# One recurrent-attention and feed-forward kernel, its written order, load queues, engines and PSUM banks changed

## The chip, the core and the metric

The kernel runs on one core of one Trainium2 chip. The metric is device time in microseconds (us), the median of several executions. One more execution was taken by the hardware profiler; its span runs from the first to the last instruction. The engines are called as in the profile: PE (matmul; PEld is its weight load), DVE, ACT, POOL and SP. SP computes nothing and only issues transfers; "ACTq", "SPq" and "POOLq" are the issuing of transfers by ACT, SP and POOL.

## The reference

Two parts follow each other. With batch 4, 8 heads, 768 steps and head size 48:

```python
for t in range(S):
    cur = einsum(u * k[t], v[t])                     # per batch and head, 48 x 48
    y[t] = einsum(r[t], state + cur)
    state = w[t][..., None] * state + einsum(k[t], v[t])
...
h = x @ w_in                                         # x is y: 3072 tokens x 384; w_in 384 x 1024
sm = softmax(h); solu = h * sm
ln = (solu - mean(solu)) / sqrt(var(solu) + 1e-6) * g_ln
out = ln @ w_out                                     # 1024 x 384
```

All inputs and the output are float32.

## The kernel before

The steps are cut into 6 chunks of 128; a chunk of one batch is a *unit*. There are 24 units, number 4c + b for chunk c and batch b. Each unit passes the same stages, each a short word in a text that is called ORDER: the word's letters name the stage, its digits the unit, and what follows the dot names an engine, a queue or a PSUM bank.

- Loads: `LW`, `LK`, `LR`, `LV` bring w, k, r and v of one unit, 192 KB each, as 1024 runs of 192 bytes. `LI0` to `LI2` bring the thirds of w_in (512 KB each), `LO0` and `LO1` the halves of w_out (768 KB each). With no letter SP issues the transfer, with `.a` ACT, with `.g` POOL (line 120). Each of w, k and r, v has a ring of 7 buffers, so a load of unit i waits until unit i - 7 has been used.
- Attention: `lw` (ACT, logarithm of w), `cum` (PE, running sums), `ex` (ACT, exponentials in PSUM), `kp` (DVE, k and r scaled by them), `krk` and `krr` (PE, transposes), `kr` (their copy, on ACT or DVE), `M` (PE, scores) and `m` (masked copy), `S`, `et`, `st` (state), `p`, `q`, `dg`, `dv` (the term with u; POOL and DVE), `vb` (v in bfloat16), `Y` and `y` (attention output), `X` and `xT` (its transpose).
- Feed-forward: `H` (PE, 24 matmuls with w_in), `e` (ACT, exponential), `he` (DVE, h * e), `hq` (its square), `Oa` and `Ob` (PE, the product with w_out in two halves, and column sums), then small steps and `o`, `out` (the store). The weights are prepared once: `wi` casts w_in, `gw` scales w_out by the gain in 8 parts (0 to 3 are the half of `LO0`), `mn` and `mc` make the column mean, `ce` subtracts it, part by part. `Oa0` needs `ce` of parts 0 to 3. `hot` is a run of matmuls without use for the result.
- Late units (16 to 23) take some transposes by transfer (`kt`, `xt`, `ht`, all from SP).

No loop sets the order. Lines 593 to 596 walk through ORDER and issue each word as it stands there; line 84, which the profile names for nearly all instructions, is the helper that records each engine's instructions in just that order:

```python
for word in ORDER.split():
    word, _, how = word.partition(".")
    name = word.rstrip("0123456789")
    stages[name](int(word[len(name):]), how)
```

So an engine never passes over an instruction that waits. That holds for issuing too: a load with `.a` stands in ACT's stream between ACT's computations (line 270 is `load_w_out`, line 501 `hidden_exp`, the stage `e`).

One more order is made by the build and is not written in ORDER. A transfer that SP or ACT issues counts its landing on one of eight semaphores, DMAHW0 to DMAHW7. Before the next transfer on the same semaphore is issued, its engine waits until the earlier one on it has landed. POOL's transfers have semaphores of their own. Which transfer stands on which semaphore is seen in the built program; the parts that the steps below touch are, for this kernel:

```
DMAHW3: LR0 LK2.a LK4.a LR7.a LV7 LR10.a LW15 ...
DMAHW4: LW2.a LW3 LK5 LR6 LI1.a LW13 LR12 ...
DMAHW0: LW0 LR2 LK1 LW7 LR9 LK10 LR14.a ...
DMAHW2: LW1.a LV1 LR5 LW8 LK9 LW14 LK14 LW11.a ...
DMAHW7: LK0.a LR3 LW9.a LR8.a LI0.a LR11 ...
```

PSUM has 8 banks; the digit after the dot of a PE word is its first bank. `cum`, `M` and `H` take two banks. A PE word waits until the earlier contents of its banks have been read.

Of the kernel before, what the change touches and what calls it, by code (L numbers as in the profile page):

```python
# [36 lines left out]
ex11 dv8 q10 kp11 lw13 sq1 Y8.n6 krr14 qm1 qm0 ex12 H4.3 lv0 y8.d kp12 vb11.p lv1 ea3.p rs1 rs0 vb10.p ea2.p LR17
p12 o0.d sel10 krk11.6 o1.a cum13.0 kr14.d out1 dg9 hq2.a ex13 krr11 Oa3.2 kr11.d e4 out0 vb12.p q12 krk12.7 kp13
Ob3 lw15 sq3 lw17 LR16.a Oa2.5 cum15.0 krr12 qm3 he4 LK17.a p11 LK15 dv9 q11 krk13.6 Ob2 ex15 S10.3 S11.4 p14 lv3
LW21 kr12.d LV16.a rs3 kp15 LK16 LK19 sq2 et10 o3.a qm2 et11 Y9.i7 krr13 lv2 cum17.0 st10 lw16 y9.a rs2 st11 ex17  # L40
o2.a out3 ea4.p S12.2 kr13.d cum16.3 dg11 et12 H5.6 kp17 p15 ex16 st12 kp16 e5 hq4.a p13 dg10 X8.5 LW19 H7.0 vb13.p
e7 he5 H6.2 out2 e6 LV18.g dg12 he7 dv10 S13.4 LK18 Oa4.7 he6 et13 krk15.6 LR20 lw19 hq5.a Ob4 q13 M12.0 xT8.a sq4
krr15 LV15.g st13 dv12 m12.a qm4 qh13 Y10.n3 Oa5.2 M11.0 M13.4 Ob5 lv4 rs4 sel12 kr15.d LV17 o4.a q14 LV14 vb14.p
X9.7 m11.a hq6.d y10.d q15 X10.3 LW18 LR19 sq5 M14.0 m13.d ea6.p lw18 LK20 dv11 xT9.d qm5 LR22.a cum19.4 lv5 xT10.d
hq7.d rs5 H8.6 m14.d sel11 dg13 dv13 o5.a ex19 e8 LK22.a kp19 H9.2 out4 ea7.p Oa6.0 cum18.4 LW20 he8 e9 Ob6 LR18
S14.6 Y11.n7 lw20 ea9.p ex18 he9 sq6 p16 qm6 kp18 out5 lv6 H10.1 rs6 o6.d hq9.a et14 dg14 st14 e10 dv14 Y12.n4
Oa7.0 y11.d LW22 y12.d vb16.a cum20.5 hq8.a ex20 q16 Ob7 ea8.p LK21 sq7 kt16 vb15.a dg15 he10 kt17 lw22 kp20 qm7
p17 Y14.n3 Oa9.7 X11.4 xT11.a lv7 q17 out6 y14.d rs7 S16.2 Y13.n1 ea10.p y13.d et16 Ob9 o7.a M15.3 sq9 kt18 st16
qm9 m15.a M17.0 LW23 M18.5 Oa8.2 m17.d M16.3 lv9 cum22.0 rs9 o9.a vb17.a LK23 out7 p19 LV21 hq10.a ex22 out9 m18.d
Ob8 m16.d qh16 dg16 LV19 dg17 kt19 H11.5 sq8 lw21 Oa10.3 X12.4 p20 e11 qm8 kp22 xT12.a lv8 X13.7 xT13.d dv15 he11  # L50
dv17 sel15 q20 Ob10 rs8 sq10 q19 o8.a qm10 lv10 rs10 out8 X14.4 H12.0 Y17.n7 Y15.n2 xT14.d e12 dv16 hq11.a H13.5
e13 o10.d ea11.p y15.d he12 y17.d LR23 p18 out10 LV22 he13 vb18.p ea12.p hq12.a H14.3 Y16.n7 LR21 Oa11.0 q18
cum21.1 Ob11 e14 qh19 y16.d ex21 vb19.d he14 sq11 p22 hq13.a S15.6 qm11 kt22 lv11 rs11 dg18 dv18 o11.a Oa12.7 et15
X15.5 Ob12 ea13.p kt20 sq12 kp21 M19.3 xT15.d p23 qm12 xt16 lv12 st15 Y18.n2 H15.0 rs12 out11 ea14.p LV23 o12.a
dg20 m19.d lw23 e15 y18.d ea15.p dg19 he15 H16.6 dv19 out12 Y19.n5 cum23.2 Oa13.4 vb23.p hq14.a xt17 kt21 S17.0
ex23 kp23 q23 Ob13 p21 q22 LV20 xt18 vb21.a e16 sq13 Oa14.1 qm13 H17.2 kt23 lv13 y19.d et17 rs13 o13.a he16 sv16
vb20.p M21.4 hq15.a e17 M20.6 st17 out13 Ob14 sq14 dg23 m20.d Oa15.0 dv23 qm14 vb22.p m21.a S19.7 Ob15 xt19 he17
ht16 q21 lv14 rs14 o14.a sel21 sq15 qm15 lv15 et19 M23.3 m23.d out14 dv20 M22.1 ht17 rs15 H18.5 qh21 m22.a dg21
o15.a out15 e18 dv21 Y20.n4 y20.d dg22 xt20 hq16.a Y21.n2 S18.1 et18 y21.d dv22 hq17.a sel22 he18 H19.3 xt21 st18
Oa16.0 Oa17.2 e19 st19 ht18 hq18.a Y22.n1 Ob16 sq16 y22.d Ob17 he19 qm16 lv16 xt22 sq17 H21.5 sv18 Y23.n7 qm17  # L60
Oa18.4 sv17 rs16 lv17 rs17 e21 o16.d ht19 hq19.a o17.d H20.0 y23.d out16 e20 Ob18 sq18 out17 he21 xt23 H22.5 qm18
# [565 lines left out]
```

## Time and profile before

| what | value |
|---|---|
| median of 3 executions | 156.16 us (154.19 to 156.34) |
| profiled execution's own time | 151.6 us |
| its span | 149.7 us |
| mean granted PE clock | 0.966 |
| busy: PE, DVE, ACT, POOL | 130.6, 122.3, 122.1, 116.0 us |
| moved by transfers | 31.50 MB, mean 210 GB/s |

The page gives, in tenths, how busy each engine was in 40 equal slices of the span, the clock granted to PE, and the mean busy share of the 16 DMA engines. The view of windows gives busy time by engine in stretches that one names. The timeline lists instructions with start and duration; a bracket at a line's end gives the idle time before it and what ended it.

### The profile page before, as it was taken

Reading aid. Unit: us, or ns where it says so; the run is one execution under the profiler, and the core shown is the slowest. Engines: PE = TensorE matmul, PEld = TensorE weight load, DVE = VectorE, ACT = ScalarE, POOL = GpSimd, SP = SyncE. Lnnn points to the kernel's source line nnn. Section 1 sums busy time; section 2 is a strip of 40 time slices with the busy share of each in tenths; the row PEclk is TensorE's granted clock in tenths of the full one; section 3 lists DMA queues with packets and bytes.
Section 4 is the critical chain, followed back from the end, with each engine's and each line's share of the span. In section 5 each row is a group of like instructions: output and inputs, shape, how many; then the busy total and the mean of one; then the engine's idle time right before and its main releaser. Section 6 shows DMA issues by size and latency. Waiting matters only on the chain. (4 is left out here: it accounts for less than half of the span.)

```text
span 149.7 us, 4668 instructions
## 1 busy us (share of the span) xinstructions
PE 130.6 (87%) x1804; PEld 95.3 (64%) x1809; DVE 122.3 (82%) x211; ACT 122.1 (82%) x266; POOL 116.0 (77%) x147
## 2 busy tenths in 40 slices
PE   6957439787599989999999999999999999899970
...
PEclk9999975899959999999999999999999999999999
DMA  5999999999999899989998999895978687479342
GB/s 104 255 287 262 278 239 210 246 286 316 362 322 254 174 204 226 204 215 246 244 239 180 224 220 217 174 203 146 198 184 185 119 194 210 100 173 166 88 158 105
DMA packets 112199, 31.50 MB, mean 210 GB/s; under 512 B 107161, under 2 KB 111266, under 8 KB 112178
## 3 DMA queue, kind: packets, MB, share of 16 engines
q1 hardware_dynamic: 91426, 24.26, 74.1%
q10 hardware_dynamic: 20048, 4.79, 14.3%
q0 software_dynamic: 704, 2.16, 4.4%
...
## 5 line engine op out<-in xcount | busy, mean ns | idle before, releaser
L84 PE MATMUL ps<-w,he 128*128 128x385 bf16 x192 | 42.4, 325 | 0.7 <-DVE st L84 0.4
L84 DVE TENSOR_TENSOR kp<-ps,kr_in 128x768 bf16<-128x768 f32 x24 | 22.9, 952 | 11.0 <-ACT ps L84 6.9
L84 POOL TENSOR_TENSOR p<-kr_in 128x384 bf16<-128x384 f32 x24 | 23.9, 1003 | 4.6 <-DMA kr_in<-in_k_dram 3.6
L84 PE MATMUL ps<-xT,win_sb 128*128 128x128 bf16 x432 | 27.0, 220 | 0.0
L84 POOL TENSOR_TENSOR ea<-e 128x512 bf16<-128x512 bf16 x15 | 17.7, 1184 | 11.0 <-ACT e L84 11.0
L84 PEld LDWEIGHTS <-win_sb 128*128 128x128 bf16 x432 | 25.2, 99 | 0.7
L84 ACT ACTIVATE e<-ps 128x1024 bf16<-128x1024 f32 x24 | 24.4, 1020 | 0.9 <-PE ps L84 0.8
L84 ACT ACTIVATE ps<-ps 128x768 f32<-128x768 f32 x24 | 19.1, 802 | 6.1 <-PE ps L84 6.0
L84 PE MATMUL ps<-one_col,hq 128*128 128x1 bf16 x144 | 23.6, 164 | 0.0
L84 DVE TENSOR_TENSOR he<-ps,e 128x1024 bf16<-128x1024 f32 x18 | 21.7, 1216 | 1.5 <-ACT e L84 1.4
L84 POOL TENSOR_TENSOR q<-p,u_bc 128x384 bf16<-128x384 bf16 x24 | 22.5, 939 | 0.2
L84 PEld LDWEIGHTS <-he 128*128 128x128 bf16 x192 | 18.0, 96 | 7.1 <-DMA he<-win_f 1.3
L84 DVE TENSOR_TENSOR m<-ps,keep 128x1024 bf16<-128x1024 f32 x18 | 21.7, 1216 | 0.4 <-PE ps L84 0.4
L84 POOL TENSOR_TENSOR dv<-vb,dg 128x384 bf16<-128x384 bf16 x24 | 19.9, 832 | 1.9 <-DVE dg L84 1.2
L84 PEld LDWEIGHTS <-kp 128*128 128x128 bf16 x208 | 13.9, 101 | 6.2 <-DVE kp L84 2.2
L84 ACT ACTIVATE lw<-w_in 128x384 bf16<-128x384 f32 x24 | 12.4, 525 | 4.2 <-DMA w_in<-in_w_dram 4.2
L84 PEld LDWEIGHTS <-kr 64*128 64x128 bf16 (+1 forms) x272 | 11.0, 97 | 6.2 <-issue 2.7
L84 PEld LDWEIGHTS <-hq 128*128 128x128 bf16 x144 | 11.2, 96 | 5.6
L84 ACT ACTIVATE hq<-he 128x1024 bf16<-128x1024 bf16 x13 | 13.7, 1053 | 0.0
L84 PE MATMUL ps<-ident,kp 128*128 128x128 bf16 x128 | 11.6, 231 | 1.6 <-DVE kp L84 1.6
L84 DVE TENSOR_REDUCE dg<-q 128x8 f32<-128x384 bf16 (+1 forms) x24 | 11.9, 500 | 0.4 <-POOL q L84 0.4
L84 PE MATMUL ps<-lw,uti_neg 128*128 128x384 bf16 x24 | 8.2, 344 | 3.2 <-DVE m L84 1.2
...
## 6 DMA issues: line engine op xcount, KB each, us to landing
...
```

The costliest lines, as they stand in the source:

```text
L84: made = make(*args, **kwargs)
```

## The change

Only ORDER is written anew. All stages are the same, and the sizes of the rings too. What differs:

- Loads by queue: of the 96 loads of w, k, r, v, SP issues 71 (66 before), ACT 19 (as before, but other ones, 16 of them ahead of `e0` where it was 12) and POOL 6 (11 before). All five transfers of w_in and w_out (`LI`, `LO`) come from ACT; before, ACT issued `LI0` and `LI1` and SP the rest.
- The order of the loads and of the units (`kp` runs 0 1 2 3 6 4 5 7 8 9 10 13 11 12 ... instead of 0 1 2 3 5 4 7 6 8 9 10 14 11 12 ...).
- Engines: `kr` 13 on DVE and 3 on ACT (10 and 6), `m` 16 and 8 (18 and 6), `xT` 6 and 10 (10 and 6), `o` 11 and 13 (8 and 16), `vb` 14 on POOL and 10 on ACT (11 and 12, one on DVE), `gw` 3 on POOL and 5 on ACT (1 and 6, one on DVE), all three `wi` on POOL (2, one on ACT), small shifts of `ce`, `y`, `sel` and `qh`.
- `hot`: 20 matmuls in six words instead of 18 in four. PSUM banks are given anew.

The start of ORDER, up to the first words of the feed-forward part:

```diff
-LW0 ih0 LW1.a LW2.a LU0 LR0 LG0 LK0.a lw0 hot13.0 cum0.0 LR1 LK1.a LR2 LK2.a ex0 LV1 LW3 LV2.g LW4 LW5 ik0 lw2 kp0
-us0.4 lw1 p0 cum1.5 LR3 LK3 uc0 ex1 cum2.0 kp1 ex2 LV3.g krk0.2 p1 kp2 q0 hot3.3 krk1.6 vb1.a LV0.a krr0 lw3 LR5
...
-xT1.a vb6.a st1 S3.1 M4.2 LI1.a X0.0 q5 kp7 et3 p6 cum6.4 xT0.d gs0.7 p7 ex6 Y2.i6 dg4 m4.d S4.0 gc0 vb8.a M5.2 LV7
-lw8 kp6 Y3.i7 y2.a q6 LI2 krk7.4 st3 y3.a dv4 krk6.5 vb5.a cum8.6 et4 m5.d LI0.a S5.1 st4 ex8 dg5 cum9.2 LO1 ex9
-krr6 krr7 LK10 kp8 q7 kp9 kr6.a krk8.0 et5 p8 krr8 wi1.p dg6 lw10 kr7.d X2.5 vb7.p LR10.a xT2.a kr8.a S6.6 Y4.i3
-dg7 X3.5 xT3.d S8.7 et6 st5 y4.a dv5 LO0 S7.5 et8 et7 wi2.a LW14 st6 M6.3 Y5.i2 st8 M7.6 cum10.0 LW13 dv7 m6.d
-wi0.p y5.a m7.d LR14.a ex10 X4.2 LV9.g st7 H0.3 xT4.d krk9.5 LV10 q8 LW12 qh8 LR11 gw7.a gw5.a dv6 LV13.g H1.6 LK12
-LK14 kp10 e0 gw6.a Y6.n0 he0 krk10.1 krr9 X5.2 gw4.a gw2.d e1 gw0.a krr10 gw1.a gw3.p p10 y6.d xT5.d he1 kr9.d p9
...
+LR0.a LK0.a LW0 LR1.a LW1 lw0 hot10.0 cum0.0 lw1 cum1.2 LV0.a ex0 ex1 LR3.a LV3.g ik0 kp0 LV5.g LV4.g LU0 LR2.a LK1
+vb3.a us0.4 LW2 LV2.g LW3 uc0 lw2 lw3 LK3.a LV6.g ih0 LV1 kp1 p0 krk0.7 krr0 kr0.d krk1.0 vb0.a LW6 krr1 vb1.a
+kr1.d M0.3 cum2.6 m0.d M1.0 ex2 LW4.a hot2.2 cum3.2 S0.4 m1.d lw6 LW5.a LK2 LV7.g LK6 q0 cum6.0 ex3 kp2 ex6 p1 p2
+dg0 kp3 S1.5 hot5.6 krk3.2 krk2.3 et0 krr3 krr2 LR6 st0 LW7 vb2.p vb5.a kp6 LR4.a vb4.a et1 dv0 q2 p3 LR5 st1
+krk6.4 lw4 krr6 Y0.i5 LK5.a LK7.a cum4.6 lw7 lw5 ex4 LK4 LW8 kr3.d kr2.d y0.a LR7 kr6.d dg2 S2.0 et2 q1 q3 cum7.3
+cum5.1 LK8.a dg1 dv1 p5 ex5 S3.5 kp4 krk4.7 LW13 LI2.a krr4 st2 vb6.a X0.6 kp5 p6 ex7 hot1.0 M3.0 vb7.p p4 xT0.a
+et3 dg3 kr4.d q5 q4 LW9 dv2 m3.a sel3 dv3 qh5 S5.2 LK10 kp7 M4.6 m4.d lw13 LK9.a S4.3 LG0 krk5.4 lw9 LR8 et5 Y1.i1
+krr5 lw8 et4 st3 st5 gs0.7 kr5.d LW14.a M2.5 st4 m2.d LW10 p7 dg4 dv4 y1.a hot1.0 X1.4 lw10 LI1.a xT1.a gc0 cum8.0
+cum9.2 ex8 ex9 hot1.4 krk7.5 krr7 LR10 LR9 q7 wi2.p LW11 lw11 cum10.6 S7.4 ex10 LI0.a kp8 Y3.i0 Y2.i1 y2.a kr7.d
+kp9 kp10 et7 st7 LW12 dg5 krk8.5 cum13.2 krr8 y3.a lw12 LR13 X3.1 lw14 X2.0 LK13 M5.6 xT3.a xT2.a M6.0 ex13 LK12.a
+LV9 LK11 kr8.d p10 dv5 p8 m5.d wi1.p Y4.i4 M8.5 krk9.7 kp13 m6.a LV10 krr9 LO1.a M7.0 S6.2 wi0.p y4.a m8.d m7.d
+kr9.a et6 cum11.3 LR11 cum12.5 Y5.i7 ex11 LR12 ex12 st6 y5.a H0.0 X4.7 kp11 LV8 vb10.a sel6 q8 q6 krk10.4 LO0.a e0
+M9.2 vb8.p vb9.p kp12 xT4.a dg7 LK14 m9.d krr10 H2.5 LW15 kr10.a p11 qh8 LR14 LV11 X5.7 he0 dv7 H1.2 krk11.0 LV13
+dg6 q10 dv6 gw7.p krk13.4 e2 LW16 he2 gw4.a gw0.p e1 krr11 Y7.i1 cum14.5 LW20 kr11.d krr13 xT5.a krk12.7 S9.0 y7.a
+he1 kr13.d gw6.a gw1.p S8.1 ex14 gw5.a dg8 krr12 kp14 et8 Y6.n2 et9 LK17 LR15 H3.3 kr12.a gw2.a LV14 gw3.a X7.7
+LW17 e3 st9 dv8 st8 vb11.p M11.5 Y8.n0 xT7.d mn0.1 p9 m11.a y6.d mc0 S11.2 lw15 ce6.d he3 ce1.p ce0.p ce4.d ce2.d
+ce5.d LK15 et11 LK16 M12.5 H4.3 ce3.p st11 m12.a ce7.d M10.5 krk14.7 hq0.a q9 hq1.a S10.2 Oa0.1 hq3.a LV12 lw16
...
```

The semaphores of the changed program are given out anew by the build. Those on which ACT's loads stand:

```
DMAHW1: LW1 LV0.a LW7 LW13 LK7.a LK13 LI1.a LW16 ...
DMAHW2: LR0.a LV1 LK3.a LW9 LR10 LV9 LV8 LW20 LO0.a LK18 ...
DMAHW3: LU0 LW6 LR5 LR4.a LR9 LK11 LK14 LK12.a ...
DMAHW4: LK0.a LK2 LK4 LK10 LK8.a LK9.a LW15 ...
DMAHW6: LR1.a LK6 LW8 LR8 LW12 LW14.a LI0.a LO1.a LW18 ...
DMAHW7: LW2 LR2.a LR7 LK5.a LI2.a LR11 ...
```

The built program has, in ACT's stream, `LO0.a` directly ahead of `e0`, and `LO0.a` waits on DMAHW2 until eight transfers on it have landed, the eighth of which is `LW20`.

More of the change, by code (lines that the diff above doesn't have):

```diff
@@ L27 @@
-dg3 krk4.3 Y1.i6 LR8.a p5 krk5.7 lw9 krr4 krr5 cum7.4 dv3 m3.d y1.a X1.6 ex7 q4 LV5.g kr5.a kr4.d dv2 LR9 LK8 LK9
-xT1.a vb6.a st1 S3.1 M4.2 LI1.a X0.0 q5 kp7 et3 p6 cum6.4 xT0.d gs0.7 p7 ex6 Y2.i6 dg4 m4.d S4.0 gc0 vb8.a M5.2 LV7
-lw8 kp6 Y3.i7 y2.a q6 LI2 krk7.4 st3 y3.a dv4 krk6.5 vb5.a cum8.6 et4 m5.d LI0.a S5.1 st4 ex8 dg5 cum9.2 LO1 ex9
-krr6 krr7 LK10 kp8 q7 kp9 kr6.a krk8.0 et5 p8 krr8 wi1.p dg6 lw10 kr7.d X2.5 vb7.p LR10.a xT2.a kr8.a S6.6 Y4.i3
-dg7 X3.5 xT3.d S8.7 et6 st5 y4.a dv5 LO0 S7.5 et8 et7 wi2.a LW14 st6 M6.3 Y5.i2 st8 M7.6 cum10.0 LW13 dv7 m6.d
@@ L32 @@
-wi0.p y5.a m7.d LR14.a ex10 X4.2 LV9.g st7 H0.3 xT4.d krk9.5 LV10 q8 LW12 qh8 LR11 gw7.a gw5.a dv6 LV13.g H1.6 LK12
-LK14 kp10 e0 gw6.a Y6.n0 he0 krk10.1 krr9 X5.2 gw4.a gw2.d e1 gw0.a krr10 gw1.a gw3.p p10 y6.d xT5.d he1 kr9.d p9
-dg8 kr10.a LW15 H3.3 e3 mn0.0 mc0 LR12 ce6.d Y7.i2 hq0.a H2.5 vb9.p y7.a lw14 ce4.d he3 ce0.p ce3.d ce2.d M10.1
-LW11.a ce7.p ce5.p M9.3 S9.7 m10.a et9 m9.d ce1.p LK11 st9 LR15 cum14.0 e2 lw12 hq1.a he2 LV11.g Oa0.2 M8.3 Ob0
-X7.7 ex14 m8.d LV12 kp14 q9 hq3.d lw11 xT7.a Oa1.5 LW16 LR13.a cum11.3 X6.7 Ob1 xT6.d LK13 sq0 LW17 cum12.0 krk14.7
@@ L37 @@
[L37 to L61, printed above, removed]
@@ new lines @@
+krr14 LW21 Ob0 LW18 sel11 p12 m10.d sel12 et10 sq0 q11 y8.d dg9 LR16 Oa1.0 e4 LW19 ea2.p dg10 qm0 cum16.5 LR17 lv0
+kr14.d lw17 p13 st10 Ob1 rs0 ex16 sq1 Oa3.7 hq2.a he4 o0.d cum15.3 LK18 q12 qm1 dv10 Ob3 kp16 ex15 cum17.1 out0 sq3
+lv1 ex17 qm3 lv3 p15 ea4.p H5.5 LV16 kp15 kp17 rs1 dv9 rs3 o1.a q13 o3.d Oa2.3 X6.4 krk15.0 Ob2 e5 p16 xT6.d hq4.a
+Y10.n2 sq2 vb12.a X8.1 he5 qm2 lv2 dg11 rs2 o2.a krr15 Y9.n7 LV15 dg12 H6.4 dv11 Y11.n3 out1 lw21 y9.d vb14.p dv12
+kr15.d xT8.a p14 q15 out3 M14.0 vb13.p lw19 e6 ea6.p LK20 H7.6 LV18 out2 ea5.p dg13 q14 y10.d hq5.d Oa4.2 m14.a
@@ new lines @@
+vb15.p he6 e7 lw18 M13.0 m13.a sel14 M15.4 y11.d LW22.a Ob4 Y12.n3 he7 sq4 m15.d lw20 ea7.p qm4 y12.d LR18 cum18.6
+sel13 ex18 S14.0 S12.1 et14 p17 kp18 S13.5 lv4 rs4 vb16.p LR19 LR22 et13 st14 H8.3 LK19 X9.6 et12 st13 st12 o4.a
+Oa5.2 hq6.a e8 cum20.0 ex20 p18 LK21 dg15 he8 LR21 Ob5 xT9.d sq5 Oa6.7 ea8.p dv13 qm5 lv5 LR20 kp20 lw22 cum21.4
+rs5 Ob6 ex21 cum19.0 S15.6 o5.d sq6 qm6 hq7.a out4 lv6 H9.2 kp21 kt16 rs6 o6.d ex19 LW23 et15 e9 kp19 Oa7.5 X10.4
+out5 xT10.a X11.7 xT11.d he9 Ob7 S16.4 hq8.a Y13.n7 q16 cum22.0 sq7 et16 qm7 lv7 ea9.p H10.2 rs7 y13.d q18 Oa8.7
@@ new lines @@
+LV17 ex22 dv15 out6 o7.a LK22 dg14 st15 st16 hq9.d LV19 kt17 H11.4 kp22 out7 Ob8 X13.1 e10 Oa9.0 X12.6 e11 sq8 he10
+qm8 ea10.p he11 LV21.a dv14 lv8 xT13.a ea11.p Ob9 xT12.d q17 p19 M17.1 rs8 o8.a LK23 dg16 vb19.p kt19 sq9 qm9
+vb17.a lv9 rs9 o9.a out8 m17.d hq11.a p21 LV23 M16.3 H13.5 e13 hq10.a m16.d Y15.n0 out9 Y14.n7 y14.d LR23 H12.1
+he13 Oa11.4 e12 X14.7 Ob11 dg17 y15.d lw23 q19 dv16 ea13.p vb18.p sq11 qm11 he12 hq13.a xT14.a kt18 dv17 Oa10.5
+lv11 p20 Y16.n6 y16.d p22 Ob10 Y17.n1 X15.0 M18.6 q20 kt21 rs11 sq10 kt20 o11.d hq12.a qm10 y17.d lv10 rs10 out11
```

18 lines of the change are left out of this document (12 added, 6 removed).

## The prediction

> **What bounds the kernel now.** I read the slices first, then the windows split where `H0` starts on PE (43.4) and where the last `Ob` starts (143.8), then the queues, then the timeline of ACT and POOL around ACT's issues.
>
> ```profile
> PE   6957439787599989999999999999999999899970
> PEclk9999975899959999999999999999999999999999
> DMA  5999999999999899989998999895978687479342
> ```
> ```profile
> 0.00:43.40 43.40, 30.84 (x340) 19.26 (x342) 30.74 (x62) 27.94 (x55) 35.07 (x56) 0.89 1.09 263
> 43.40:143.80 100.40, 98.58 (x1456) 75.39 (x1458) 90.68 (x147) 92.23 (x203) 80.92 (x92) 1.00 0.90 192
> 143.80:149.70 5.90, 1.15 (x13) 0.61 (x10) 0.92 (x4) 1.90 (x8) 0.00 (x0) 1.00 0.36 133
> ```
> ```profile
> q1 hardware_dynamic: 91426, 24.26, 74.1%
> q10 hardware_dynamic: 20048, 4.79, 14.3%
> q0 software_dynamic: 704, 2.16, 4.4%
> ```
> ```profile
> 38.20 0.41 ACTq L84 DMA_DIRECT2D kr_in<-in_r_dram  x1
> 38.65 0.48 ACT L84 COPY xT<-ps 128x384 bf16<-128x384 bf16 x1 [2.34 <-DMA v_in<-in_v_dram]
> ```
> ```profile
> 38.18 0.51 POOL L84 CAST vb<-v_in 128x384 bf16<-128x384 f32 x1 [1.82 <-DMA v_in<-in_v_dram]
> ```
>
> (Window columns: stretch, length, busy PE, PEld, DVE, ACT, POOL, granted clock, share of the 16 DMA engines, GB/s. Queue q1 is SP's, q10 ACT's, q0 POOL's.)
>
> Two stages have two bounds. Up to 43.4 the DMA engines are full (share 1.09) and PE is busy for 30.84 of 43.40: loads decide when units are ready. From 43.4 on PE is busy for 98.58 of 100.40 and decides; the last 5.9 are the chain from the last product to the last store. Matmul ends are modelled, so I checked PE by the steps from one word's first weight load to the next word's: medians are 1.39 for `H`, 0.84 for `Oa`, 0.92 for `Ob`, 0.33 for `M`, 0.41 for `Y`. With these medians 98.4 us of PE work stand in ORDER from `H0` on; the trace took 100.4. So: end = time at which a PE word starts + work ordered from it on + 5.9, give or take 2.
>
> The third fact is how ACT issues. `LR10.a` goes out at 38.20, when ACT has sat idle for 2.34, and what ended the wait is a v transfer: `LV7`, landed at 38.12, the transfer ahead of `LR10.a` on its semaphore, DMAHW3. POOL starts the cast of that v at 38.18. The same pairs by the trace's landings: `LW9.a` issued 16.89, `LR3` landed 16.82; `LI1.a` 28.66, `LR6` 28.64; `LR14.a` 42.24, `LK10` 42.11; `LW11.a` 53.10, `LK14` 53.09. A load in ACT's stream thus holds ACT until an earlier transfer, often SP's, is down.
>
> **The change part by part.** *Pace of the DMA engines.* From the trace's packet records a 192 KB load from SP or ACT costs the 16 engines 0.98 us (1024 packets x 15.3 ns / 16), one from POOL 0.60 (q0: 4.4% of 149.7 = 6.6 for 11), a third of w_in 1.37, a half of w_out 2.2. In these units 20.0 were down at 20 us, 30.4 at 30, 39.7 at 38.1, 52.5 at 50, 58.4 at 57 and 63.9 at 60.6 (51 loads, 9 of POOL's, 3 thirds, 2 halves). I read times in the changed kernel off this table.
>
> *Five loads fewer on POOL.* POOL saves 5 x 0.94 = 4.7 us of issuing, and the engines pay 5 x 0.38 = 1.9 more, all after the first six loads that both kernels have early. Beside the rest by 60 us; I take 0, bounds -1.9 to +1.9. The Trainium skill's page DMA: Bandwidth & Descriptors, section Issuing engine by pattern, calls transfers of SP and ACT "generally faster"; the rows have POOL's at 0.60 against 0.98 in engine time, so here the measurement decides, and by the page the 1.9 would be a gain instead of a cost.
>
> *Order of loads, no holds yet.* The last of k and r for unit 9, `LR9`, has 42.6 of DMA work at its end (22 SP loads, 15 of ACT, 6 of POOL, two thirds of w_in), down at about 41; before, `LK9` was down at 35.34. Behind it DVE runs `kp9`, `kp10`, `st7`, `dg5`, `kr8`, `m5`, `kp13`, `m8`, `m7` = 0.95+0.95+0.55+0.54+0.68+1.22+0.95+1.22+1.22 = 8.3, and `H0` takes the banks that `m7` reads: 49.3 at the earliest, 43.4 before. PE has 97.4 left from `H0`, 1.0 less than before.
>
> *The holds on ACT.* `LK12.a` waits for `LK14`: 33 SP loads, 15 of ACT, 6 of POOL and w_in, 54.7 of work, down at about 53. That is late for ACT but the loads run on meanwhile. The one that decides is `LO0.a`, which stands directly ahead of `e0` and waits for `LW20`, the 39th load of SP. Ahead of that landing stand 39 + 16 loads of 0.98, 6 of 0.60, three thirds (4.1) and `LO1.a` (2.2): 63.8, so 60.6 by the table. If `LK12.a`, `LI0.a` and `LO1.a` run late, only 59.2 stand ahead: 57.5; if ACT's stops leave semaphores idle and the engines run dry, some 64. `e0` therefore starts near 61, not near 45.4 as before, and `he0` (1.22) ends near 63.3, since `e` takes 1.02. Queued behind on ACT: `xT4`, `kr10`, `e2`; behind `he0`, PE's `krk11`, which takes bank 0 from `H0`. PE can do `H0`, `H2`, `H1` meanwhile and stands at `krk11` with 91.9 left.
>
> *The half of w_out.* `LO0.a` issued at 60.7 lands after 7.1 (the row of transfers of w_out), 67.8. POOL then scales two parts (2 x 1.27) to 70.3, PE makes the mean (1.17), ACT copies it (0.49), POOL centres three of the four parts that `Oa0` needs (3 x 0.88): 74.6, and with the waits between engines 75. PE's own work from `krk11` to `Oa0`, 10.4, would end at 73.7, so this chain is the later by a little. From `Oa0` 81.5 are left on PE.
>
> *Sum.* 75.0 + 81.0 (81.5 without the last `Ob`) + 5.9 = 161.9, against a span of 149.7: +12.2. Before, the same sum with `Oa0` at 55.1 and 88.1 left is 148.6. `LW20` at 57.5 gives +9.1, at 64 +15.6.
>
> *Engines, banks, warm-up.* Rows times counts give DVE -0.1, ACT -4.0, POOL +1.3 over the kernel (`kr` 3 x 0.68 on DVE for 3 x 1.01 on ACT, `m` two to ACT, `o` three to DVE, `xT` four to ACT, `vb` three to POOL); beside PE in the dense stage, 0. If PE's cover were gone, ACT's 4.0 would be the gain. `hot10` for `hot13` lets `cum0` start 3 x 0.43 = 1.3 earlier, but `kp2` then waits for `LK2`, which was 9th among the loads and is now 22nd: 0. The clock is granted at 0.7 and 0.5 in slices 6, 7 and 12; a longer idle PE may add one such dip, 5 x (1 - 0.66) = 1.7 by the window from 40 to 45, or save it: plus or minus 1.7. Later holds (`LW22.a`, `LV21.a`, `LV20.a`) cost 0 to 2.3 each by `LR10.a`'s row; by then loads run ahead: 0. The last words are the same: 5.9.
>
> **The rivals.** *Order only.* The holds cost nothing because ACT reaches `LO0.a` after `LW20` is down. Then `H0` at 49.3 + 97.4 + 2 + 5.9 = 154.6, +4.9, 161.1 us. For it: four of the five holds in the trace of before show no idle ACT. Against: `LR10.a` does, and ACT needs only the work ahead of `e0`, 32.1 of busy rows, to be there.
>
> *No difference (not slower).* Queues only name who issues; the engines serve all alike and units come as early as before. Place: the first 45 us; price: 1.0 less PE work from `H0`, so -1.0 to 0, 155.2 us at the low end. It decides if `LW20` is down when `e0` could start, at 45.4 as before: 63.8 of work by then is 1.41 per us, against 1.05 in the table. For it: the full first stage moves 263 GB/s and slices with large packets 362. Against: the order puts 42.6 of work ahead of the end of unit 9's loads, which were down at 35.34 before, about 37 by the table. The Trainium skill's page DMA: Bandwidth & Descriptors, section Issuing engines are not separate DMA queues, says that issuing from several engines saves only sequencer time; the share near 1.0 with all three queues agrees, but by that rule alone the time would stay.
>
> *ACT was the bound.* ACT is at 92.23 of 100.40 in the dense stage; if it and not PE paced it, 4.0 less work gives 152.2 us. Against: PE's 98.58.
>
> **How the numbers follow.** The sum is made in the profiled execution (151.6 us, span 149.7), and the median of the runs, 156.16, lies 4.6 above it; I add the difference to the median: 156.2 + 12.2 = 168.4 us. Chances: the hold decides 0.65, order only 0.20, no difference 0.11, ACT as the bound 0.04. The range must leave out no more than 0.2: from just under order only, 159.5, up to the late hold with one more dip of the clock, 156.2 + 15.6 + 1.7, about 174. It leaves out the last two cases and a little above. The likeliest case's own range is 164 to 173. About 2% is what a measurement of this kernel tells from no change (the three runs lie 1.4% apart). Slower by over 2% (above 159.3): the first two cases, 0.85. Within 2%: 0.11. Faster: 0.04.
>
> **What would show it.** In the changed kernel's profile: ACT idle for several us just ahead of the first `e` (128x1024), ended by a w transfer, with ACT's issue of `wout_f` at 60 to 61; before it a stop near 53 at ACT's issue of a k transfer; the first matmul with `win_sb` near 50, a gap on PE after the first three `H`, and the first product with `w` of the feed-forward near 75; then a PE as dense as before to the end. If ACT's `wout_f` issue comes by 50, or the first `e` follows `H0` at once, the hold is wrong. If the DMA share stays near 1 and `LW20` lands much before 57, the table of pace is wrong.

## The result and the profile after

The kernel after takes 165.07 us (median of 4 executions, 164.18 to 167.12). The kernel before, with one execution more than the prediction had, takes 155.18 us (152.16 to 156.34). The ratio is 1.076, 95% interval 1.057 to 1.095: slower, as forecast (168.4 / 156.16 = 1.078). The medians lie 9.9 us apart. The profiled execution took 164.2 us, span 162.3, against 151.6 and 149.7 before: +12.6, where the sum had +12.2. The profiled execution of after has the lowest mean clock of the four, 0.880, and the shortest time; the other three have 0.914 to 0.922 and take 164.95 to 167.12 us. Comparisons leave disturbed executions out, so that some experiments below have no ratio; among those left out are the profiled one of e5 and all but the profiled one of e3.

The slices of the kernel after, the same three rows as before's:

```profile
PE   6647865994975949978999999999999899999980
PEclk9985555576598796999999999999999999999998
DMA  5999999999999979079269899899995956465933
```

A slice is 4.06 us here; slices are counted from 0. PE becomes dense only from slice 19 (77 us) on; before it was so from slice 11 (41 us). The DMA row has a hole that it lacked before: slice 16 (64.9 to 69.0) is at 0, while PE is busy in it. SP had stopped for 8.1 us ahead of `LK16`, which takes the buffer of unit 9: `p9`, the last to read that buffer, ended on POOL at 69.10, and `LK16` went out at 69.13. The clock granted to PE is at 0.5 to 0.7 through slices 3 to 10.

The windows, split where `H0`, `krk11` and `Oa0` start and where the last `Ob` starts:

```profile
0.00:43.40 43.40, 30.80 (x238) 18.21 (x241) 26.02 (x55) 21.61 (x44) 31.40 (x52) 0.66 1.13 249
43.40:54.50 11.10, 8.27 (x114) 5.96 (x113) 8.01 (x11) 7.12 (x15) 7.05 (x9) 0.81 1.08 259
54.50:62.40 7.90, 5.84 (x98) 5.51 (x96) 4.64 (x6) 4.13 (x8) 3.86 (x6) 0.93 0.94 226
62.40:76.00 13.60, 12.04 (x194) 10.16 (x191) 10.96 (x18) 12.90 (x23) 10.72 (x12) 0.89 0.66 144
76.00:156.80 80.80, 80.08 (x1163) 60.03 (x1164) 73.22 (x121) 70.60 (x169) 63.21 (x72) 1.00 0.82 164
156.80:162.30 5.50, 1.07 (x12) 0.57 (x10) 1.08 (x4) 1.81 (x7) 0.00 (x0) 0.87 0.38 143
```

The stage ahead of `H0` grew from 43.4 to 54.5 at the same DMA share (1.13 and 1.08 against 1.09). In the first 43.4 us PE recorded 238 matmuls where before had 340, and was busy as long (30.80 and 30.84): at a granted clock of 0.66 against 0.89 each took longer. In the units of the prediction's table of pace, more loads were down at 43.4 than before (47.1 against 44.2), but fewer units were ready. Then come 7.9 us with PE busy for 5.84 and 13.6 with 12.04; each of these two has one gap on PE:

```profile
60.73 0.33 PE L85 MATMUL ps<-ident,y 128*128 128x128 bf16 x3 [2.06 <-ACT xT L85]
73.47 1.50 PE L85 MATMUL ps<-xT,win_sb 128*128 128x128 bf16 x24 [1.56 <-DVE he L85]
```

The first is `X5`, which waits for `xT4`, queued on ACT right behind `e0`. From `Oa0` on PE has 0.7 idle in 80.8, and the tail is 5.5.

The queues:

```profile
q1 hardware_dynamic: 95426, 23.15, 70.6%
q10 hardware_dynamic: 21248, 6.88, 16.5%
q0 software_dynamic: 384, 1.18, 2.1%
```

POOL's queue went from 704 packets to 384 (11 loads to 6), ACT's from 4.79 MB to 6.88.

The timeline of ACT, at the two places that the prediction named:

```profile
49.60 0.47 ACTq L85 DMA_DIRECT2D kr_in<-in_k_dram  x1
50.11 1.01 ACT L85 CAST m<-ps 128x1024 bf16<-128x1024 f32 x1 [2.20 <-POOL win_sb L85]
...
58.72 0.46 ACTq L85 DMA_DIRECT2D wout_f<-in_moe_w_out_dram  x1
59.29 1.02 ACT L85 ACTIVATE e<-ps 128x1024 bf16<-128x1024 f32 x1 [3.67 <-DMA w_in<-in_w_dram]
```

`LO0.a` is issued at 58.72, when `LW20` has landed at 58.70, and `e0` follows after 3.67 us of idle ACT: that is the hold as forecast. At `LK12.a` the bracket names POOL's `win_sb` (ended 49.94), but `m6` does not use it, and the built program has it wait for PE alone. ACT had stopped at the issue just ahead (49.60) until `LK14` was down (49.52), and `m6` stood behind that issue. PE's `M7`, which takes the banks that `m6` reads, then waited for `m6`, and `H0` came 3.3 later:

```profile
51.17 0.40 PE L85 MATMUL ps<-kr 64*128 64x128 bf16 x8 [1.99 <-ACT m L85]
```

Eleven holds of this kind stand ahead of `H0`, and here the prediction had looked too little. In the built program of before, the earlier transfer on a semaphore stands 8 to 59 words *earlier* in ORDER than the load of ACT behind it, for all such loads ahead of `e0`. In after it often stands *later* (`LR3.a` and `LW4.a` are on DMAHW5, `LW5.a` on DMAHW0, two semaphores that the list ahead of the prediction lacks):

```
LR3.a behind LK1 (8 words later in ORDER)   LK5.a behind LR7 (11)    LW14.a behind LW12 (41)
LR2.a behind LW2 (4)                        LK7.a behind LW13 (27)   LI1.a behind LK13 (40)
LK3.a behind LV1 (3)                        LK8.a behind LK10 (34)   LK12.a behind LK14 (51)
LW5.a behind LR6 (20)                       LR4.a behind LR5 (6)     LO0.a behind LW20 (38)
```

The semaphores are handed out in the order in which the build goes through the transfers, and there SP's, which wait for little, run ahead of ACT's. So ACT waits for transfers that are not wanted until long after. Ahead of `H0` ACT stands idle for 25.8 us in after, 18.6 of them at these eleven loads; before, it was 14.7.

### The profile page after: what moved, and what is told of

The parts are those of the page before. It is cut to its first block, busy times and chain, and to the rows that moved or that the text cites. A ratio compares the mean times of both kernels' runs of the same rounds, so it can differ in the third digit from the quotient of the medians.

```text
span 162.3 us, 4663 instructions
## 1 busy us (share of the span) xinstructions
PE 138.1 (85%) x1805; PEld 100.4 (62%) x1810; DVE 123.9 (76%) x211; ACT 118.2 (73%) x261; POOL 116.2 (72%) x148
## 3 DMA queue, kind: packets, MB, share of 16 engines
q10 hardware_dynamic: 21248, 6.88, 16.5%
q0 software_dynamic: 384, 1.18, 2.1%
## 4 chain that ended last, share of the span: by engine, by line
PE 48%; DMA 20%; ACT 10%; DVE 7%; SPq 5%; issue 4%; POOL 2%; ACTq 1%; DVEq 0%; POOLq 0%
PE ps L85 48%; DMA v_in<-in_v_dram 5%; SPq L85 5%; DMA w_in<-in_w_dram 4%; DMA kr_in<-in_k_dram 4%; DMA he<-win_f 3%; DMA kr_in<-in_r_dram 2%; DMA xT<-y 2%; DVE he L85 2%; ACT w L85 1%; DVE m L85 1%; ACT e L85 1%; ACT ps L85 1%; ACT m L85 1%; POOL p L85 1%
## 5 line engine op out<-in xcount | busy, mean ns | idle before, releaser
L85 PE MATMUL ps<-w,he 128*128 128x385 bf16 x192 | 41.9, 325 | 0.2 <-DMA he<-win_f 0.2
L85 POOL TENSOR_TENSOR dv<-vb,dg 128x384 bf16<-128x384 bf16 x24 | 20.4, 852 | 13.8 <-DVE dg L85 13.7
L85 PE MATMUL ps<-xT,win_sb 128*128 128x128 bf16 x432 | 27.5, 221 | 1.6 <-DVE he L85 1.6
L85 POOL TENSOR_TENSOR p<-kr_in 128x384 bf16<-128x384 f32 x24 | 24.4, 1020 | 1.4 <-DMA kr_in<-in_k_dram 1.4
L85 DVE TENSOR_TENSOR m<-ps,keep 128x1024 bf16<-128x1024 f32 x16 | 19.4, 1217 | 4.8 <-PE ps L85 4.2
L85 PEld LDWEIGHTS <-he 128*128 128x128 bf16 x192 | 18.1, 96 | 6.3 <-DMA he<-win_f 0.4
L85 POOL TENSOR_TENSOR q<-p,u_bc 128x384 bf16<-128x384 bf16 x24 | 21.8, 914 | 0.1
L85 PEld LDWEIGHTS <-kp 128*128 128x128 bf16 x208 | 16.4, 116 | 7.6 <-DVE kp L85 4.9
L85 PE MATMUL ps<-ident,kp 128*128 128x128 bf16 x128 | 13.2, 260 | 3.0 <-DVE kp L85 3.0
L85 PE MATMUL ps<-kr 64*128 64x128 bf16 x192 | 9.7, 231 | 4.2 <-ACT m L85 2.0
L85 PE MATMUL ps<-lw,uti_neg 128*128 128x384 bf16 x24 | 10.0, 418 | 3.7 <-ACT lw L85 3.7
```

What stands on the lines that cost most here:

```text
L85: made = make(*args, **kwargs)
```

## The experiments

Theory A, stated ahead of them: the loss has two parts, the holds behind transfers that stand later in ORDER, and the order of the loads. Theory B: all of it is holds. Theory C: order of the computation, engines and banks. Starts by the profiled execution, in us:

| kernel | H0 | e0 | krk11 | mn0 | Oa0 | last Ob | span | ratio to before (95%) |
|---|---|---|---|---|---|---|---|---|
| before | 43.4 | 45.4 | 62.8 | 49.3 | 55.1 | 143.8 | 149.7 | 1 |
| after | 54.5 | 59.3 | 62.4 | 69.6 | 76.0 | 156.8 | 162.3 | 1.076 (1.057 to 1.095) |
| e1 after, semaphores in order | 49.9 | 51.4 | 59.4 | 65.3 | 71.8 | 152.9 | 158.4 | 1.036 (1.025 to 1.047) |
| e4 after, one hold off | 54.2 | 56.0 | 59.6 | 65.4 | 72.0 | 152.6 | 158.1 | 1.038 (1.026 to 1.051) |
| e12 after, LO0 on SP | 55.5 | 57.0 | 60.7 | 66.5 | 73.1 | 153.9 | 159.4 | 1.048 (1.036 to 1.060) |
| e7 e1, two units earlier, LO1 later | 50.6 | 52.2 | 55.8 | 65.0 | 72.8 | 154.4 | 159.9 | none; 161.63 against 154.01 |
| e9 e1, two units earlier | 48.9 | 52.2 | 55.1 | 62.2 | 68.7 | 149.4 | 154.9 | 1.030 (1.023 to 1.037) |
| e8 e1, five v loads on POOL | 51.1 | 53.3 | 56.9 | 63.8 | 71.2 | 152.0 | 158.3 | none; 160.89 against 154.01 |
| e10 after, twelve loads on SP | 52.3 | 55.4 | 63.3 | 69.2 | 75.8 | 156.6 | 162.1 | 1.068 (1.062 to 1.073) |
| e11 e10 and units earlier | 52.9 | 57.4 | 60.3 | 67.2 | 73.6 | 155.1 | 160.7 | 1.053 (1.048 to 1.058) |
| e2 before, weights on ACT | 48.4 | 57.4 | 80.9 | 61.6 | 67.2 | 162.2 | 168.1 | 1.114 (1.100 to 1.127) |
| e3 e2, semaphores in order | 44.2 | 46.1 | 63.5 | 50.3 | 56.0 | 144.1 | 150.0 | none; 158.14 against 154.30 |
| e5 before, semaphores in order | 45.9 | 47.7 | 65.6 | 51.5 | 57.4 | 151.2 | 157.1 | none; 156.69 against 154.01 |
| e6 before with after's loads, in order | 51.4 | 60.6 | 84.1 | 65.6 | 71.7 | 165.7 | 171.3 | none; 172.41 against 154.01 |

(`krk11` stands later in before's ORDER than in after's, so it is compared within a family only. The median of before beside e1 to e4 was 154.30, e5 to e8 154.01, e9 to e11 154.37, e12 154.82; beside after 155.18. The helper's line is 83 in the experiments and 85 in after.)

**e1: all holds behind later transfers off.** The edit, in the helper that records each engine's instructions, ties each transfer of SP and ACT to the one before it in ORDER, for the build's order alone:

```diff
             self.last = made.ins
+            if name.startswith("dma_start") and self.engine is not self.tc.nc.gpsimd:
+                before = getattr(self.tc.nc, "last_transfer", None)
+                if before is not None:
+                    self.tc.add_manual_dep(made.ins, before.name, mybir.DependencyInfo(
+                        mybir.DependencyClass.NoSync, mybir.DependencyReason.DATA))
+                self.tc.nc.last_transfer = made.ins
             return made
```

> The changed kernel with every word, queue, engine and bank as it is; only the build is told to give out the eight landing semaphores in the order of ORDER, so that each load waits for the one eight places ahead of it in ORDER and no longer for one that stands behind it. Theory A (the holds on ACT and the order of loads share the loss): LO0.a goes out before H0, H0 starts at 48 to 50 instead of 54.5, e0 right after it, span 153 to 156 (before 149.7, changed 162.3). Theory B (the holds are all of it): H0 near 43 to 44, span 148 to 150. Theory C (the order of loads and the engines decide, holds only fill time that ACT would have waited anyway): H0 stays past 53, span 160 to 163.

Measured: 159.45 us (157.95 to 160.28). `e0` follows `H0` at once, `H0` starts at 49.9: the prediction's "order only" had 49.3. What ACT now waits for ahead of `H0` is its own input, the w transfers of the `lw` words, 16.6 us in nine stops (3.1 before, 3.8 in after):

```profile
ACT lw L83 <- DMA w_in<-in_w_dram: 16.6, 9, 3.9
```

About half of the loss went. But the span is 2.4 above theory A's upper end, and DVE and POOL show what holds it between `H0` and `krk11`. The timeline of DVE in e1:

```profile
51.78 0.96 DVE L83 TENSOR_TENSOR kp<-ps,kr_in 128x768 bf16<-128x768 f32 x1 [2.05 <-DMA kr_in<-in_r_dram]
54.00 0.96 DVE L83 TENSOR_TENSOR kp<-ps,kr_in 128x768 bf16<-128x768 f32 x1 [1.27 <-DMA kr_in<-in_r_dram]
```

The timelines of PE and of POOL in e1:

```profile
55.02 2.21 PE L83 MATMUL ps<-xT,win_sb 128*128 128x128 bf16 x24 [1.18 <-DVE kp L83]
```
```profile
56.44 0.95 POOL L83 CAST vb<-v_in 128x384 bf16<-128x384 f32 x2 [5.90 <-DMA v_in<-in_v_dram]
```

`kp11` and `kp12` wait for `LR11` (landed 51.66) and `LR12` (53.92), `H2` waits for `kp12`, whose banks it takes, and POOL waits 5.90 for `LV8` (56.39) ahead of its parts of w_out. No hold of ACT makes these transfers late in e1. But with the same ORDER they had landed earlier in after, at 46.0, 48.0 and 48.8: there SP's loads had passed the ones that ACT held back. So e1 does not only take ACT's holds away; it brings ACT's loads forward, and SP's come later for it.

**e2 and e3: before, with w_in and w_out on ACT.** In e2 `LI2`, `LO1`, `LO0` get `.a`; e3 is e2 with the helper of e1.

```diff
-LI2 ... LO1 ... LO0
+LI2.a ... LO1.a ... LO0.a
```

> The kernel before with LI2, LO1 and LO0 moved from SP's queue to ACT's at their places in ORDER, nothing else. The build then pairs LO1.a behind LW14, LR14.a behind LK11 and LW11.a behind LR15, all of which stand later in ORDER; LR14.a is ahead of ex10 and e0. Theory A and B (holds): e0 comes at 50 to 52 instead of 45.4, span 153 to 157. Theory C: the order of loads is the same, span 149 to 151.

> As e2, with the semaphores given out in the order of ORDER. Theories A and B: no hold on ACT that matters, span 148 to 151, so issuing the weights from ACT costs nothing in itself. If issuing them from ACT costs by itself: 153 or more, like e2.

e2 took 171.76 us, far more than either theory had. Three letters make the build hand the semaphores out otherwise, and `LR14.a` now stands behind `LK11`, 71 words later in ORDER. ACT in e2:

```profile
55.10 0.46 ACTq L83 DMA_DIRECT2D kr_in<-in_r_dram  x1
55.69 0.80 ACT L83 ACTIVATE ps<-ps 128x768 f32<-128x768 f32 x1 [7.52 <-DMA kr_in<-in_k_dram]
```

`LK11` landed at 55.03, `LR14.a` went out at 55.10, and ACT stood for 7.52 with `e0` behind it. `LO1.a`, behind `LW14` (37 words later), had stopped ACT for 2.58 before. `e0` is 12.0 late and `krk11` 18.1, more than the stops themselves; how the rest adds up was not followed. In e3, with the same letters and the semaphores in order, the profiled execution is before's again (span 150.0, `Oa0` 56.0). Its other three executions lie at 156.6 to 159.7, still far under e2's lowest, 170.0; so e3 shows that the loss of e2 is the holds, and whether the weights on ACT cost a per cent or two is not settled.

**e4 and e12: the one hold ahead of `e0`, taken off in two ways.** e4 ties only `LW20` behind `LO0.a` in the build's order, so that `LO0.a` comes to stand behind `LW15`, which landed at 51.51; `LK12.a` and `LO1.a` change their places on the semaphores too, but go out as in after (49.33 and 50.03). e12 leaves the build alone and takes a letter away:

```diff
-LO0.a e0
+LO0 e0
```

> The changed kernel with one edge for the build: LW20 takes its semaphore after LO0.a. LO0.a then waits for LW15 instead of LW20, LK12.a for LV8 instead of LK14; all other pairs ahead of e0 but LO1.a's (LK14) stay. Theory A and B: e0 follows H0 within 2 us (56 to 57 instead of 59.3), Oa0 2 to 4 earlier, span 158.5 to 161, so this one hold is worth some 2 to 3 of the 12.6 and the earlier ones the rest. Theory C: span as before that, 162 to 163.

> The kernel after with one letter taken away: LO0 is issued by SP at its place in ORDER instead of by ACT, semaphores as the build hands them out. ACT's hold ahead of e0 (3.67 us, behind LW20) is gone by the queue this time and not by the way the semaphores are handed out; eleven of the twelve loads that the experiment with twelve loads on SP moved stay with ACT, so that the pace of the loads should stay as in after (58.7 us of engine time down at 55; in that experiment 54.0). The holds ahead of H0 stay. Theory A: e0 at 55 to 57 instead of 59.3, H0 at 53.5 to 55 as in after, Oa0 at 71 to 73, span 157.5 to 160, as in the experiment that handed out one semaphore otherwise (158.1). If that experiment's gain came from the other way of handing out alone: span 161.5 or more.

ACT in e4, and then in e12:

```profile
54.46 0.37 ACTq L83 DMA_DIRECT2D wout_f<-in_moe_w_out_dram  x1
54.83 0.52 ACT L83 CAST vb<-v_in 128x384 bf16<-128x384 f32 x1
55.96 1.02 ACT L83 ACTIVATE e<-ps 128x1024 bf16<-128x1024 f32 x1 [0.62 <-DVE dg L83]
```
```profile
56.61 0.53 ACT L83 CAST vb<-v_in 128x384 bf16<-128x384 f32 x1
57.04 1.02 ACT L83 ACTIVATE e<-ps 128x1024 bf16<-128x1024 f32 x1
```

In both, `e0` runs without the stop and `Oa0` comes 4.0 and 2.9 us earlier, though `H0` is as late as in after (54.2, 55.5). So without this hold 2.9 to 4.2 us of span go; by the medians 3.8 and 4.9, and no execution of e4 or e12 is as slow as one of after. e12 has a little less because its build puts `LI0.a` behind `LV10`, 41 words later, where ACT stands for 3.46 and `H0` comes 1.0 later than in after. The spans are near the expected ones (158.1 for 158.5 to 161, 159.4 for 157.5 to 160).

Only part of this is PE's waiting. The stop at `X5`, 2.06, is gone. The rest is mostly the clock: from `krk11` to `mn0` PE has no gap in either kernel, but the same words take 7.2 us in after and 5.8 in e4 (5.8 in e12, 5.9 in e1). Windows of after, then of e4:

```profile
62.40:69.60 7.20, 7.20 (x121) 6.39 (x119) 6.31 (x10) 6.50 (x14) 6.44 (x7) 0.80 0.40 104
```
```profile
59.60:65.40 5.80, 5.80 (x120) 5.26 (x118) 5.80 (x10) 5.80 (x13) 5.80 (x7) 1.00 0.86 171
```

The granted clock is 0.80 in the one and 1.00 in the other; that the stop brought the low clock about is not shown.

The expectation for e4 gave the earlier holds the rest of the 12.6, and that did not come out. e1, with all of them off, has `H0` 4.6 earlier than after and still meets e4 at `krk11` (59.4, 59.6) and at `Oa0` (71.8, 72.0): in e1 PE waits 1.24 and 1.18 behind `kp11` and `kp12`, whose loads are late there, and in e4 it has no gap on that stretch.

**e7 and e9: the loads of units 11 and 12 earlier.** Both are e1 with five or six words moved:

```diff
-LK12.a LV9 LK11 ... LV10 ... LO1.a ... LR11 ... LR12 ... LV8 ... LO0.a e0
+LK12.a LK11 LR11 ... LR12 LV10 LV8 LV9 ... LO1.a ... LO0.a e0      (e9)
+LK12.a LK11 LR11 ... LV10 LR12 LV8 LV9 ... LO0.a LO1.a e0          (e7)
```

> The kernel after with semaphores in the order of ORDER, as in the first experiment, and in it the k and r of units 11 and 12 moved ahead of the v of 8, 9 and 10 among SP's loads, and the half of w_out of LO1 behind LO0. In the first experiment LR11 landed at 51.7 and LR12 at 53.9, DVE stood idle 2.05 and 1.27 for them, and H2 waited for kp12, which reads its banks. Theory A: LR11 lands at 47 to 49, LR12 at 50 to 51.5, both waits go, krk11 starts at 55 to 57 instead of 59.4, span 154 to 156.5, ratio to before 1.01 to 1.03; H0 stays at 49 to 50.5, since the loads ahead of it are the same. Theory C (engines, banks and clock): krk11 within 1 us of 59.4 and the span within 1 of 158.4.

> The kernel after with semaphores in the order of ORDER; in it the k and r of units 11 and 12 and then the v of 10 stand ahead of the v of 8 and 9 among SP's loads, and LO1 stays where it was. In the experiment that moved LO1 back as well, krk11 came at 55.8, 3.6 earlier than in the first experiment (59.4), but ACT then stood idle 3.4 for LO1 ahead of gw4, and Oa0 came at 72.8 instead of 71.8: the chain from the halves of w_out over gw, mn, mc and ce set it. Theory A (LR12's landing and then that chain, both fed by late loads): krk11 at 55.5 to 57.5, no idle ACT for LO1, POOL's gw0 starts at 57 to 59.5 instead of 61.3, Oa0 at 67.5 to 70, span 153.5 to 156.5. Theory C (something common to all forms of the kernel after, as ACT's and POOL's work around e0, pins Oa0): Oa0 again at 71 to 73, span 157 to 160.

e7's first half came true: no wait for `LR11` or `LR12`, `krk11` at 55.8. Its second did not. ACT and PE in e7:

```profile
58.98 0.61 ACT L83 ACTIVATE w<-wout_f,gr 128x384 bf16<-128x384 f32 x1 [3.37 <-DMA wout_f<-in_moe_w_out_dram]
```
```profile
60.92 0.38 PE L83 MATMUL ps<-ident,kp 128*128 128x128 bf16 x4 [3.12 <-ACT xT L83]
```

`LO1`, moved behind `LO0`, landed at 58.96; `gw4` waited for it on ACT, and `xT5` and with it PE waited behind `gw4`. The 3.6 us were given back, and the span of 159.9 lies outside theory A's 154 to 156.5. e9 leaves `LO1` where it was: POOL's three parts of w_out (`gw7`, `gw0`, `gw1`) start at 58.7 instead of 61.3, `mn0` at 62.2 instead of 65.3, `Oa0` at 68.7 instead of 71.8, span 154.9, as theory A had it. By all executions the gain is smaller: 158.35 against 159.45 us, ratios 1.030 and 1.036 with intervals that overlap; the profiled one was e9's fastest and e1's slowest. Theory C's common pin at 71 to 73 is gone by the trace; the size of the gain, 1 to 3.5 us, stays open.

**e8: five loads back on POOL.** e1 with `.g` on `LV8`, `LV9`, `LV10`, `LV11`, `LV13`.

> The kernel after with semaphores in the order of ORDER, and the v of units 8 to 11 and 13 issued by POOL again, so that 11 loads are POOL's as in before. By the packet records a load from POOL takes 0.60 of engine time, one from SP or ACT 0.98. Theory A with the term as predicted (0, bounds -1.9 to +1.9): span 156.5 to 159, the gain at most 4 loads by 0.38 ahead of LR12 and LO0, 1.5 us. If POOL's sequencer decides (each issue holds it 0.9 us between its casts and products), slower than the first experiment by 1 to 4.

160.89 us and span 158.3, no gain and no loss that can be told. `krk11` comes 2.5 earlier than in e1, and POOL's own stream shows where that goes:

```profile
56.84 0.93 POOL L83 DMA_DIRECT2D v_in<-in_v_dram  x1
57.79 0.84 POOL L83 TENSOR_TENSOR dv<-vb,dg 128x384 bf16<-128x384 bf16 x1
58.56 0.92 POOL L83 DMA_DIRECT2D v_in<-in_v_dram  x1
...
61.19 3.70 POOL L83 TENSOR_SCALAR w<-wout_f,gr 128x384 bf16<-128x384 f32 x3
```

Two issues of 0.93 and 0.92 stand ahead of `gw7`, `gw0`, `gw1` in POOL's stream, and the three parts start at 61.19, as in e1 (61.28); `Oa0` keeps 0.7 of the 2.5. The Trainium skill's page DMA: Bandwidth & Descriptors, section Issuing engine by pattern, calls the transfers of SP and ACT generally faster; here neither side won.

**e5 and e6: before, with semaphores in order, and with after's loads.** e5 is before with the helper of e1. e6 is e5 with the loads of after, their queues and nearly their order (17 had to be moved), put among before's computation.

> The kernel before with one thing altered: the eight landing semaphores are handed to the transfers of SP and ACT in the order of ORDER; order, queues and engines stay. Its own holds stood behind transfers 8 to 60 words earlier in ORDER, and only LR10.a showed 2.3 us of idle ACT ahead of it. Theory A (holds cost where the earlier transfer stands later in ORDER): nothing to win here, span 147 to 151, ratio to before 0.98 to 1.01, H0 at 42 to 45. Theory B (every hold costs, and handing out in order helps any kernel): 3 us or more less, ratio under 0.98. If the time rises by over 2%, the way the semaphores are handed out has a price of its own, and the reading of the first experiment has to be mended for it.

> The kernel before with the loads of the kernel after (queues, order, and place among the computation where rings and first uses allow; 17 loads had to be moved), semaphores in the order of ORDER; computation, engines and banks are those of before. After in that same form took 158.4 us of span, H0 at 49.9, 3.6% over before. Theory A (what is left without holds is the order of the loads: the transfers that the words around H0 need lie later): the loss comes along with the loads, span 154 to 160, ratio 1.02 to 1.05, H0 at 46 to 51. Theory C (what is left is the order of the computation, the engines and the banks): span 148 to 152, ratio under 1.015, H0 at 43 to 45.

e5 gains nothing (156.69 against 154.01 us): theory B's second half falls, before's own holds cost nothing that can be told. Its median is 1.7% higher, and e3's, with semaphores in order too, was 2.5%: such an order may have a price of its own, and so much of e1's 3.6% is not clear. Against e5, whose profiled execution is its slowest, e6 starts `H0` 5.5 later (51.4, 45.9), and 8.0 later than before does: with the same computation, engines and banks, after's loads make `H0` late once semaphores go in order, as A had it and C had not. But the time, 172.41 us, is beyond both. ACT in e6:

```profile
51.15 0.39 ACTq L83 DMA_DIRECT2D wout_f<-in_moe_w_out_dram  x1
59.53 0.62 ACT L83 ACTIVATE w<-wout_f,gr 128x384 bf16<-128x384 f32 x1 [7.61 <-DMA wout_f<-in_moe_w_out_dram]
59.69 0.38 ACTq L83 DMA_DIRECT2D wout_f<-in_moe_w_out_dram  x1
```

Before's computation has `gw7` and `gw5` on ACT ahead of `e0`, and with after's loads `LO1` lands at 59.51 where in e5 it landed at 43.82. Order of loads and order of computation are made for each other; e6 shows the direction, and its size is no measure of after's.

**e10 and e11: twelve of ACT's loads on SP.** `LR3`, `LR2`, `LK3`, `LW5`, `LR4`, `LK5`, `LK7`, `LK8`, `LW14`, `LI1`, `LK12`, `LO0` lose their `.a`; e11 has e9's order of loads too. The build hands out the semaphores, and no hold of ACT behind a later transfer is left.

> The kernel after with twelve of ACT's loads given to SP, each at its place in ORDER (LR3, LR2, LK3, LW5, LR4, LK5, LK7, LK8, LW14, LI1, LK12, LO0). The semaphores are handed out as the build does it; the holds of ACT's loads that are left stand behind transfers 6 or more words earlier in ORDER. Theory A (holds of ACT behind later transfers, and nothing else about ACT's queue): like the first experiment, which took the holds away by another way of handing out semaphores: H0 at 48 to 51, e0 without an idle ACT ahead of it for a w transfer, span 155 to 160, ratio to before 1.02 to 1.045. If the gain of the first experiment came from the other way of handing out and not from the holds: span 161 or more.

> Both edits together: twelve of ACT's loads on SP, and the k and r of units 11 and 12 and the v of 10 ahead of the v of 8 and 9; semaphores as the build hands them out. Theory A: as the experiment with the units earlier and semaphores in order, span 153 to 157, ratio 1.00 to 1.03, and no better than before, since the loads ahead of H0 (some 42 us of engine time against 36 in before) are the same: H0 at 48 to 51. A time under before's would speak against the order of loads as the rest of the loss.

Theory A fails here: 164.28 us and a span of 162.1, almost after's, and that is what was set down for the case that e1's gain came from the handing out and not from the holds. e12 speaks against that case, since it has the build's own handing out and keeps its gain. `e0` is free of a hold (ACT's stop for a w transfer is gone), but everything comes later. Windows of e1, then of e10:

```profile
20.00:40.00 20.00, 13.17 (x169) 9.18 (x171) 15.38 (x24) 10.25 (x23) 17.89 (x21) 0.88 1.13 251
```
```profile
20.00:40.00 20.00, 11.85 (x144) 7.81 (x144) 15.89 (x24) 8.91 (x21) 16.33 (x20) 0.88 1.02 212
```

From 20 to 40 us the transfers move 212 GB/s where e1 moves 251. In the units of the table of pace 41.6 us of work are down at 43.4, in e1 45.5, in after 47.1; `LR9` lands at 43.86, in e1 at 38.96. So the gain of the freed ACT was paid back by slower loads. e12, which moves only `LO0`, keeps the pace better (46.1 at 43.4) and keeps the gain. From 20 to 40 us SP spends 18.7 us on issuing in e10 and 17.5 in e1, ACT beside it 0.7 (2 transfers) and 2.7 (6); by 40 us 45 loads are issued in e10, 49 in e1 and 53 in after. So SP's stream is nearly full in both, and what ACT issued beside it is missing in e10. That this sets the pace is likely and was not tried.

e11 missed its range too: span 160.7 and ratio 1.053, for 153 to 157 and 1.00 to 1.03. Against e10 the earlier units gain 1.4 us of span, and `H0` stays late (52.9).

## Why the prediction came out as it did

The direction and the place were right, and the size was near: +12.6 in the profiles for +12.2, +9.9 by the medians. The hold that carried the forecast is a cause, but of a quarter to a half of the loss: +8.4 to +9.7 are left without it (e4, e12), where "order only" had +4.9. Point by point:

- *Pace.* The table had 58.4 down at 57 and 63.9 at 60.6; the trace has 58.7 at 55 and 63.8 at 59, some 2 us faster, so `LW20` was down at 58.70 and not at 60.6, inside the 57.5 to 64 given. The table took the loads to land in the order of ORDER; in after SP's passed those held on ACT, and `LR9` was down at 35.46, not at about 41.
- *The hold ahead of `e0`.* `e0` at 59.3 for about 61. e4 and e12 show that it is a cause and not only a sign: without it 2.9 to 4.2 us of span go. It reached PE by another way than forecast: PE was to do `H1` meanwhile and to stop at `krk11` for `he0`, but it stopped at `X5`, ahead of `H1`, for `xT4` on ACT, and `he0` was done (61.57) when `krk11` came (62.4). The prediction had 7.3 between its "order only" and its sum; e1, all holds off, finds 3.9 in the profiles and 1.0757 / 1.0363 = 1.038 in the ratios, 6 us. The hold's price was set against a stage that would else run on freely; in e4 `H0` is still late by the other holds, and in e1 `LR11`, `LR12` and `LV8` are late.
- *The holds of before.* Four of five were said to show no idle ACT. Of these four `LW9.a` shows some: 1.26 us that ended with `LR3`, the transfer it stood behind.
- *The holds ahead of `H0`.* A step that failed: `LK12.a` was called "late for ACT but the loads run on meanwhile", that is 0, and the ten others were not looked at. Together they stopped ACT for 18.6 us and put `H0` at 54.5 instead of 49.3; e1 without them has 49.9. It cost the sum nothing, because `e0` was held past `H0` anyway.
- *Order of the loads.* In after itself it did not make `H0` late: `LR9` landed at 35.46, as early as before's `LK9` (35.34), and the holds did the rest. Without holds `LR9` was to land at about 41 and `H0` to start at 49.3; e1 has 38.96 and 49.9. That is near by two errors: the landing came 2 us earlier, and DVE's chain behind it took 10.3 for 8.3, since `kp10` waited for ACT and ACT for `LW11`. What was missed is the part behind `H0`: `LR11`, `LR12` and `LV8` land at 51.7 to 56.4 in e1 and hold `kp11`, `kp12`, `H2` and POOL, which explains much of why its span is 158.4 and not 154.6; e9 moves five words and has 154.9.
- *The half of w_out.* It landed at 64.35 and not at 67.8: 5.6 us after its issue, not the 7.1 of before's row; between 60.2 and 63.4 no other load came down. POOL's two parts ended at 66.90 for 70.3, and its last centring at 74.28 for 74.6, so this chain did not set `Oa0` as forecast. PE had no gap from 60.73 on until `H4`; the last parts on ACT, `gw2` and `gw3`, ended at 69.36, just ahead of `mn0` (69.62). `H4` then waited 1.56 for `he3`, which stood on DVE behind `ce6` and so behind the mean. PE's own work from `krk11` to `Oa0` took 12.04 for 10.4, mostly by the low clock. Errors of opposite sign, and `Oa0` at 76.0 for 75 by luck.
- *From `Oa0` on.* 80.8 for 81.0, and a tail of 5.5 for 5.9. Spans: 162.3 for 161.9.
- *POOL's five loads, engines, banks.* 0 for POOL stands (e8), though the gain at `krk11` was mostly lost behind POOL's issues. The dense part shows no gain from ACT's lighter load.
- *Level.* The median came out 3.3 below the forecast with the span right within 0.4: the difference was added to a median of 156.16, and before's is 155.18 with one more execution, which is 1.0 of it. The rest is that before's profiled execution was a quick one, 3.6 below that median, and after's is 0.9 below its own.

Rivals: "order only" would have been 161.1, and e1 comes nearest to that kernel (1.036 x 156.16 = 161.8). "No difference" and "ACT was the bound" are excluded by the ratio's interval.

What stays open: e9 is still 3.0% over before. Its `H0` starts at 48.9 for 43.4, with ACT waiting 15.9 us for w transfers ahead of it; how much of the 3% that is, how much the order of the computation, and how much the semaphores in order (e5, e3) was not separated. And the clock granted to PE was 0.66 in the first 43.4 us of after against 0.89 before. In e9 it is 0.86 in the first 48 us and in e10 0.79; no run changed it alone. After's other executions, with a higher mean clock and no shorter time, speak against a large share of it in the total.
